# Attention and two feed-forward layers in one launch: query sums and output low parts on another engine, with a new table of positions

## The chip, the cores and the metric

The kernel runs on one core of one Trainium2 chip. The metric is the device time of one execution in microseconds. Before the change it is 699.79 us (median of 3 runs, 699.38 to 701.0).

## The reference

Three stages follow one another, all in fp32. Attention has 2 batches, 8 heads, 1152 keys and a head size of 64; neighbouring queries are averaged in pairs first, so each head has 576 of them:

```
q_pool = q.reshape(B, H, S // 2, 2, D).mean(axis=3)
scores = matmul(q_pool, k^T) / sqrt(D)
attn   = softmax(scores, axis=-1)
x      = matmul(attn, v)            -> 1152 tokens x 512
```

The first feed-forward layer takes x through 512 -> 2048 -> 512 with an ELU between, the second does the same with h * tanh(softplus(h)) between. Query and key inputs are drawn eight times larger than the values.

## The kernel before

**High and low parts.** TensorE's operands are rounded, so the kernel multiplies most operands in two parts: a high part, cast by ScalarE or GpSimd, and a low part, the difference between the value and its high part, taken by VectorE or GpSimd. Where a product needs it, the cross terms of both are added.

**Attention.** Two heads of a batch make a pair n (0 to 7). A pair has 1152 query rows over both heads, in nine tiles of 128 (tile t = 0 to 8; over all pairs s = 9n + t, 72 tiles). For each pair:

- `load_qk` and `load_v` bring the raw rows, `pool_q` (L216) adds the two queries of each pair of rows (tile `qp`, 96 x 768), `turn_q` lets TensorE transpose the sums (`psq`, L233), `split_q` (L244, L246) scales them and makes high and low parts, and `stack_q` (L248) copies them into `QH`, `QL` and `QM` by ten DMAs. The keys go the same way without the sum (`turn_k`, `split_k`, `stack_k`), the values through `split_v` (high by ScalarE L329, low by GpSimd L331).
- For each tile s, `scores` (L356) makes 1152 scores a row, 896 in the buffer `wide` and 256 in `rest`. `maxima` takes the maximum on VectorE (L363, L366), `exps` the exponentials and their sums on ScalarE (`rest` L378, `wide` L380). `turn` (L411) transposes the probabilities in three chunks, `split_a` makes high and low parts: for half of the chunks on ScalarE and VectorE (L436, L438), for the chunks in the list `PP['pool']` by a copy on ScalarE (`whole`, L426, two buffers) and two instructions on GpSimd (L226, L227). The list goes by 3t + c and has no chunk of tile 8. `values` (L451) multiplies with the values.
- At a pair's end `reciprocals` sends 1/sum through DRAM into a broadcast tile `R`, `join` (L464, L466) collects `xf`, and `finish` does three things: the product with `R` (link 0, L474, GpSimd), the high part `xh` (link 1, L476, ScalarE), and the low part `xl` (link 2, L478, VectorE).

**Weights.** The weights arrive as 64-bit numbers. Each 128 x 512 block is decoded by one ScalarE instruction (L602) and four of VectorE (L603, L604, L605, L607). For seventeen blocks this runs during attention, and the result is stored to DRAM and loaded again later; a few more are decoded for use at once.

**Feed-forward.** `up` (L772) and `down` (L792) run over chunks of tokens and 16 blocks of 128 hidden columns. The first chunk of the first layer needs tokens of batch 0 only, pairs 0 to 3.

**The order of the work.** In attention the order of the instructions on every engine is written out: `run` gives each piece of work a position, counted in tiles, sorts all of them, and emits them in that order. The positions stand in the table `PP['x']`: a key such as `m` (first maximum) or `p` (the sum of a pair's queries) holds an offset that is added to s, or to 9n for a pair. Keys with `@0` hold for pair 0 and the preparation of pair 1, `@7` for pair 7. An instruction waits in its engine's queue until its inputs are there, and all behind it wait too. In the feed-forward stage the order on ScalarE and VectorE is that of emission. All DMAs are issued on SP's queue.

Of the kernel before, what the change touches and what calls it, by code (L numbers as in the profile page):

```python
# [15 lines left out]
ALU = mybir.AluOpType  # L16
# [48 lines left out]
    'pl': ['xm'],  # L65
# [72 lines left out]
class Attention:  # L138
# [77 lines left out]
    def pool_q(self, n, heads=slice(0, 2)):  # L216
        if n not in self.qp:
            self.qp[n] = self.tmp.tile([PQ, NQ, 2, D], F32, name="qp", bufs=1)
        qr = self.rawqk[n][0][:, heads]
# [665 lines left out]
```

## Time and profile before

| | |
|---|---|
| median of 3 runs | 699.79 us |
| the profiled execution | 699.27 us, span 697.2 us |
| granted TensorE clock | 0.999 |
| TensorE busy | 674.0 us, 97% of the span |
| VectorE busy | 610.8 us, 88% |
| ScalarE busy | 479.0 us, 69% |
| GpSimd busy | 267.1 us, 38% |
| chain that ended last | TensorE 59%, VectorE 18%, ScalarE 10%, DMA 6%, GpSimd 2% |

In the profile PE is TensorE's matmul, PEld its weight load, DVE is VectorE, ACT ScalarE, POOL GpSimd, and SP the engine that issues the DMAs. The span is the time from the first to the last instruction; the profiled execution's own time is 2.1 us above it. A row of a view by stretch gives start and end, the length, and then the busy microseconds of PE, PEld, DVE, ACT and POOL. A share of busy time is a mean over stages, so the rows below look at the attention stage, up to about 287 us, by itself. Matmuls overlap, so a busy TensorE isn't a TensorE at its peak. The chain of waits is followed back from the last instruction: at each step to what released it, or to the instruction before it on its engine.

### The profile page before, as it was taken

To read this page: it belongs to the slowest core of one execution; us is meant where nothing else is said; L and a number is where in the kernel's file an instruction comes from. 1 tells how busy PE (TensorE), PEld (TensorE's weight loads), DVE (VectorE), ACT (ScalarE), POOL (GpSimd) and SP (SyncE) were. 2 spreads that over 40 slices of the span, in tenths; PEclk is the share of its full clock that TensorE was granted. 3 is DMA by queue.
4 is the path that set the end of the run, shared out by engine and by line. 5 is a ranking of instruction groups with operands and counts; after the bars stand their busy time and mean duration, and the time that the engine had idled before them with its cause. 6 is when DMAs were issued, how large, how long until landed. Compare 5 with 4: busy or idle time off the path is not lost.

```text
span 697.2 us, 11870 instructions
## 1 busy us (share of the span) xinstructions
PE 674.0 (97%) x4006; PEld 602.3 (86%) x4007; DVE 610.8 (88%) x1111; ACT 479.0 (69%) x1125; POOL 267.1 (38%) x308
## 2 busy tenths in 40 slices
PE   8999999999999988999999999999989999999996
PEld 5888988888888877788889999999978999999995
DVE  5999999999999999788798887886999988888884
ACT  5999999999899989765665443666655554445443
POOL 2797788878787868352210000224130000000000
PEclk9999999999999999999999999999999999999999
DMA  6977677758675642546546666565120010001001
GB/s 175 222 186 190 186 196 203 178 130 243 183 177 151 164 128 62 184 136 210 171 149 188 186 214 206 173 191 171 47 77 17 0 46 1 0 1 47 1 0 45
DMA packets 66492, 91.24 MB, mean 131 GB/s; under 512 B 24376, under 2 KB 40832, under 8 KB 66432
## 3 DMA queue, kind: packets, MB, share of 16 engines
q1 hardware_dynamic: 66432, 90.50, 46.9%
q8 instruction: 31, 0.51, 0.3%
q14 instruction: 29, 0.24, 0.1%
HBM read 60.56 MB, written 12.88 MB: 105 GB/s over the span
## 4 chain that ended last, share of the span: by engine, by line
PE 59%; DVE 18%; ACT 10%; DMA 6%; issue 3%; POOL 2%; SPq 0%; ACTq 0%; DVEq 0%; POOLq 0%
PE acc L792 23%; PE up L772 23%; PE psv L451 4%; PE pst L411 4%; PE wide L356 3%; DVE neg L366 3%; DVE wt L605 2%; DVE tl L438 2%; DMA raw<-in_moe_w_out_dram 2%; ACT a L380 2%; DVE wt L607 2%; DMA raw<-in_moe_w_in_dram 2%; DVE wt L603 1%; ACT th L436 1%; ACT wt L602 1%
## 5 line engine op out<-in xcount | busy, mean ns | idle before, releaser
L624 POOL TENSOR_TENSOR wl<-wt,wh 128x512 fp32r<-128x512 f32 x34 | 45.3, 1342 | 194.7 <-ACT wh L622 165.6
L227 POOL TENSOR_TENSOR tl<-whole,th 128x384 fp32r<-128x384 f32 (+1 forms) x112 | 112.9, 1008 | 9.3
L772 PE MATMUL up<-xh,wl 128*128 128x384 f32 (+2 forms) x336 | 113.0, 336 | 0.0
L772 PE MATMUL up<-xh,wh 128*128 128x384 f32 (+2 forms) x336 | 112.9, 336 | 0.0
L772 PE MATMUL up<-xl,wh 128*128 128x384 f32 (+2 forms) x336 | 112.8, 336 | 0.0
L411 PE MATMUL pst<-ident,a 128*128 128x128 f32 x648 | 101.9, 279 | 8.5 <-DVE tl L438 3.2
L411 PEld LDWEIGHTS pst<-ident,a 128*128 128x128 f32 x648 | 73.3, 140 | 25.4 <-DVE tl L438 6.1
L451 PE MATMUL psv<-th,vs 128*128 128x320 f32 (+1 forms) x288 | 85.1, 317 | 1.9 <-DVE tl L438 1.6
L226 POOL TENSOR_SCALAR th<-whole 128x384 fp32r<-128x384 f32 (+1 forms) x112 | 65.2, 582 | 42.7 <-ACT whole L426 41.7
L451 PE MATMUL psv<-tl,vs 128*128 128x320 f32 (+1 forms) x288 | 79.0, 295 | 0.0
L366 DVE TENSOR_REDUCE neg<-wide 128x1 f32<-128x898 f32 x72 | 78.0, 1083 | 0.5
L380 ACT ACTIVATE a<-wide,neg 128x896 f32<-128x896 f32 x72 | 73.9, 1026 | 2.5 <-DVE neg L366 2.3
L602 ACT ACTIVATE wt<-raw 128x512 f32<-128x512 f32 x64 | 43.1, 676 | 39.7 <-DMA raw<-in_moe_w_out_dram 28.2
L745 ACT ACTIVATE e<-n 128x384 f32<-128x384 f32 x48 | 25.2, 526 | 65.0 <-DVE n L744 65.0
L772 PEld LDWEIGHTS up<-xh,wh 128*128 128x128 f32 x336 | 63.3, 189 | 4.0
L772 PEld LDWEIGHTS up<-xl,wh 128*128 128x128 f32 x336 | 63.3, 188 | 4.0
L772 PEld LDWEIGHTS up<-xh,wl 128*128 128x128 f32 x336 | 63.3, 188 | 2.2
L438 DVE TENSOR_TENSOR tl<-pst,th 128x384 fp32r<-128x384 f32 (+1 forms) x128 | 59.8, 495 | 3.4 <-ACT th L436 2.0
L792 PE MATMUL acc<-gh,wl 128*128 128x512 f32 (+2 forms) x180 | 60.4, 336 | 0.0
L451 PEld LDWEIGHTS psv<-th,vs 128*128 128x128 f32 x288 | 54.4, 189 | 4.0 <-issue 1.3
L356 PE MATMUL wide<-ks,qh 128*128 128x448 f32 (+1 forms) x160 | 57.5, 373 | 0.0
L792 PE MATMUL acc<-gl,wh 128*128 128x512 f32 (+2 forms) x168 | 56.6, 337 | 0.1
(128 smaller groups left out, 1769.1 us busy)
## 6 DMA issues: line engine op xcount, KB each, us to landing
raw<-in_moe_w_out_dram SPq DMA_DIRECT2D x32, 512.0 KB, 3.8
raw<-in_moe_w_in_dram SPq DMA_DIRECT2D x32, 512.0 KB, 4.4
w<-wt SPq DMA_DIRECT2D x40, 256.0 KB, 4.4
wt<-w SPq DMA_DIRECT2D x40, 256.0 KB, 3.1
kr<-in_k_dram SPq DMA_DIRECT2D x16, 288.0 KB, 5.2
vr<-in_v_dram SPq DMA_DIRECT2D x8, 576.0 KB, 6.1
qr<-in_q_dram SPq DMA_DIRECT2D x7, 576.0 KB, 5.0
qh<-tqh SPq DMA_DIRECT2D x28, 144.0 KB, 5.1
```

Of the source, the lines that this page charges most:

```text
L226: nc.gpsimd.tensor_scalar(hi, x, 1.0, 1.0, op0=ALU.mult, op1=ALU.mult)
L227: nc.gpsimd.tensor_tensor(lo, x, hi.bitcast(F32), op=ALU.subtract)
L356: nc.tensor.matmul(dst, w[:], x[:, cols], start=(o == 0), stop=(o == len(ops) - 1))
L366: nc.vector.tensor_reduce(neg[:], wide[:, :, :WW + 1], axis=AX.XY, op=ALU.max, negate=True)
L380: nc.scalar.activation(a[:, :2 * WW].rearrange("p (c x) -> p c x", c=2), wide[:, :, :WW], AF.Exp, bias=neg[:], accum_out=self.sums[n][:, t ...
L411: nc.tensor.transpose(ps[:, i * P:(i + 1) * P], a[:, j * P:(j + 1) * P], self.ident[:])
L438: nc.vector.tensor_tensor(l, src[:, :, x0:x0 + w], h.bitcast(F32), op=ALU.subtract)
L451: nc.tensor.matmul(ps[:, :w], self.VS[n % 2][:, h, j].rearrange("p a d -> p (a d)"), t[:, j, :w], start=(c == 1), stop=(c == 2 * NKT))
L602: lambda: nc.scalar.activation(t[:], high.bitcast(F32), AF.Abs),
L624: e.tensor_tensor(l[:], t[:], h[:].bitcast(F32), op=ALU.subtract)
L772: nc.tensor.matmul(ps[:, :z], w, x, start=(o == 0), stop=(o == len(ops) - 1))
L792: nc.tensor.matmul(ps[:, :x.shape[1]], a, x, start=(i == 0 and o == 0), stop=(i == NFF - 1 and o == 2))
```

## The change

Three edits. The list `'pl'` gets `'xl'`, which sends link 2 of `finish` (L478, the low part of the attention's output, 128 x 576, once a pair) to GpSimd. `pool_q` runs on GpSimd for pairs 1 to 7; pair 0 keeps its two half sums on VectorE. And every offset of the position table has a new value; most shift by less than half a tile.

```diff
-    'pl': ['xm'],
+    'pl': ['xm', 'xl'],
...
-        'W': -0.9652, 'R': -1.0096, 'm': -0.303, 'M': 0.3113, 'e': 0.8476, 'E': 0.6177, 'T0': 0.9667, 'T1': 0.9894, 'T2': 1.2926, 'H0': 1.2651,
-        'H1': 1.4181, 'H2': 1.8235, 'L0': 1.6365, 'L1': 1.695, 'L2': 2.0604, 'f0': 12.6577, 'f1': 13.6176, 'f2': 14.1898, 'lq': -2.6801, 'lv': 0.5421,
-        'p': 0.8401, 'sq': 6.1802, 's0': 6.5617, 's1': 9.5077, ...
...
-        ... 'jd3': 12.6342, 'rec0': 9.964, ...
+        'W': -0.8185, 'R': -0.7929, 'm': -0.1468, 'M': 0.2871, 'e': 1.0106, 'E': 0.622, 'T0': 1.0969, 'T1': 1.1479, 'T2': 1.4158, 'H0': 1.2645,
+        'H1': 1.4197, 'H2': 1.8762, 'L0': 1.5754, 'L1': 1.7679, 'L2': 2.0558, 'f0': 13.0233, 'f1': 13.4493, 'f2': 13.9188, 'lq': -2.5868,
+        'lv': 0.6571, 'p': 0.9219, 'sq': 4.0105, 's0': 6.7254, 's1': 7.815, ...
...
+        ... 'jd3': 12.403, 'rec0': 9.9947, ...
...
-        self.nc.vector.tensor_tensor(out, qr[:, :, :, 0, :], qr[:, :, :, 1, :], op=ALU.add)
+        (self.nc.gpsimd if n > 0 else self.nc.vector).tensor_tensor(out, qr[:, :, :, 0, :], qr[:, :, :, 1, :], op=ALU.add)
```

The line that `'xl'` switches is not in the diff; it stands in `finish`:

```python
(nc.gpsimd if 'xl' in PP['pl'] else nc.vector).tensor_tensor(xl, xf[:], xh.bitcast(F32), op=ALU.subtract)
```

## Rows read from the trace of the kernel before

**Rows 1.** Stretches: us, each engine's busy us (instructions), granted clock, DMA share, GB/s.

```profile
20.00:280.00 260.00, 248.10 (x1715) 219.86 (x1712) 251.10 (x430) 241.81 (x624) 206.28 (x249) 1.00 0.67 172
0.00:287.00 287.00, 271.51 (x1847) 236.16 (x1849) 270.43 (x468) 259.28 (x664) 215.25 (x269) 1.00 0.67 172
540.00:680.00 140.00, 140.00 (x704) 126.95 (x703) 120.41 (x242) 69.47 (x146) 1.29 (x1) 1.00 0.04 12
```

**Rows 2.** Chain of waits, 0 to 287 us: shares; steps (start, us, what).

```profile
by line: PE psv L451 10.6%; PE pst L411 9.9%; PE wide L356 6.8%; DVE neg L366 6.6%; issue 6.1%; DVE tl L438 5.8%; ACT a L380 4.1%; DVE wt L605 3.8%; ACT th L436 3.3%; DVE wide L363 3.1%; ACT whole L426 2.9%; PE rest L356 2.6%; DMA raw<-in_m
...
145.16 1.00 DVE neg L366
147.23 1.18 PE psv L451 x8
```

**Rows 3.** Chain of waits: its steps on the moved instructions.

```profile
16.84 0.87 DVE qp L221
46.23 1.15 DVE qp L221
...
231.20 0.82 DVE xl L478
266.75 1.28 DVE xl L478
```

**Rows 4.** Waits, 0 to 287 us: who for whom, us, times, longest.

```profile
POOL th L226 <- ACT whole L426: 41.7, 39, 3.1
PEld rest L356 <- ACT a L378: 2.9, 17, 0.2
```

**Rows 5.** VectorE by line, 0 to 287 us (| busy us, mean ns |).

```profile
L607 DVE SCALAR_TENSOR_TENSOR wt<-raw,wt 128x512 int32<-128x512 int32 x20 | 19.5, 974 | 0.1
L605 DVE SCALAR_TENSOR_TENSOR wt<-raw,wt 128x512 int32<-128x512 int32 x20 | 19.2, 960 | 0.1
L604 DVE TENSOR_SCALAR wt<-wt 128x512 int32<-128x512 int32 x21 | 13.7, 653 | 0.1
L603 DVE TENSOR_SCALAR wt<-wt 128x512 f32<-128x512 f32 x21 | 11.6, 553 | 0.0
L478 DVE TENSOR_TENSOR xl<-xf,xh 128x576 fp32r<-128x576 f32 x7 | 8.4, 1203 | 0.0
L221 DVE TENSOR_TENSOR qp<-qr 96x768 f32<-96x768 f32 x7 | 8.3, 1180 | 0.0
```

**Rows 6.** Order of time near 292 us: start, us, instruction, [idle before].

```profile
294.85 1.28 POOL L624 TENSOR_TENSOR wl<-wt,qr 128x512 fp32r<-128x512 f32 x1 [3.24 <-ACT qr L622]
...
292.36 0.76 DVE L478 TENSOR_TENSOR xl<-xf,xh 128x576 fp32r<-128x576 f32 x1 [0.42 <-ACT xh L476]
```

**Rows 7.** Groups by line, GpSimd, 0 to 287 us.

```profile
L227 POOL TENSOR_TENSOR tl<-whole,th 128x384 fp32r<-128x384 f32 x96 | 102.3, 1066 | 8.0
L474 POOL TENSOR_TENSOR xf<-xf,R 128x576 f32<-128x576 f32 x7 | 9.9, 1420 | 5.0 <-DVE xf L466 3.7 <-DMA R<-rdram 1.3
```

**Rows 8.** Order of time: GpSimd's holes, TensorE's turn of the sums.

```profile
50.85 0.51 POOL L226 TENSOR_SCALAR th<-whole 128x384 fp32r<-128x384 f32 x1 [0.81 <-ACT whole L426]
...
49.45 0.41 PE L233 MATMUL psq<-ident,qp 96*128 96x96 f32 x3
...
149.62 0.51 POOL L226 TENSOR_SCALAR th<-whole 128x384 fp32r<-128x384 f32 x1 [1.99 <-ACT whole L426]
...
150.95 0.41 PE L233 MATMUL psq<-ident,qp 96*128 96x96 f32 x3
```

**Rows 9.** Groups by line, VectorE, 385 to 435 us, where GpSimd is idle.

```profile
L605 DVE SCALAR_TENSOR_TENSOR wt<-raw,wt 128x512 int32<-128x512 int32 x14 | 9.7, 692 | 0.5
L607 DVE SCALAR_TENSOR_TENSOR wt<-raw,wt 128x512 int32<-128x512 int32 x13 | 9.0, 691 | 0.4
L604 DVE TENSOR_SCALAR wt<-wt 128x512 int32<-128x512 int32 x14 | 6.0, 427 | 0.5
L603 DVE TENSOR_SCALAR wt<-wt 128x512 f32<-128x512 f32 x14 | 6.0, 426 | 7.2 <-ACT wt L602 7.0
```

112 rows, old and new, of the table PP are left out of this document.

## The prediction

> **What bounds the kernel now.** I read the busy time by stretch first. From 540 to 680 us TensorE is busy for 140.00 of 140 us: the two feed-forward layers stream matmuls and nothing of the change is in them but one subtraction. The attention stage, up to about 287 us, is another matter: TensorE 271.51, VectorE 270.43, ScalarE 259.28 and GpSimd 215.25 busy us [rows 1]. Three engines stand within 4% of each other, so this stage has no single bound, and the share of busy time alone doesn't say what VectorE's relief is worth.
>
> Next the chain of waits over that stage. It names lines of TensorE and VectorE in turn [rows 2]; the VectorE lines that the row names (neg 6.6, tl 5.8, wt L605 3.8, wide 3.1) make 19.3% of it. In order of time it changes hands inside each pair of heads: at 145.16 us a VectorE maximum is on it, from 147.23 us TensorE streams its own work [rows 2]. So a microsecond taken off VectorE counts in some stretches and not in others.
>
> Third, which of the moved instructions stand on that chain: two of the seven sums (0.87 and 1.15 us) and two of the seven subtractions in the stage (0.82 and 1.28 us) [rows 3], 4.1 us together. Last the waits: GpSimd's largest is for ScalarE's copies of the transposed probabilities, 41.7 us in 39 places; TensorE's for the freed rest of the scores is small, 2.9 us in 17 [rows 4]. GpSimd has room, if not always at the right place.
>
> **The change part by part.** *Off VectorE.* Pair 0 keeps its two half sums there. Seven sums of 96x768 go, 8.3 us, and the subtractions of pairs 0 to 6, 8.4 us [rows 5]: 16.7 us in the attention stage. The eighth subtraction starts at 292.36 us, takes 0.76 us and comes behind an idle 0.42 us [rows 6], in the stage that TensorE streams: nothing. Of the 16.7 us, 4.1 us are on the chain. The other 12.6 us are worth something where a queue behind them reaches the chain later: between nothing and all of it. I take the 19.3% of the chain that named VectorE lines hold, 2.4 us. Sum: -6.5 us. Where it goes, TensorE's stream and ScalarE's copies are late next.
>
> *Onto GpSimd.* A subtraction has the form of the product beside it, 128x576: 1.42 us. For the sum of 768 columns no row exists. From 384 columns at 1.066 us to 576 at 1.420 us [rows 7] another 192 columns add 0.354 us, so 1.77 us; in proportion to columns it would be 1.89. I take 1.8. It reads neighbouring rows of queries in steps, and no GpSimd row shows such a read, so I keep 3.6 us, double, as the upper end. The stage gets 7 x 1.8 + 7 x 1.42 = 22.5 us, and GpSimd stands at some 238 us of it, 84%.
>
> What hides this? In the new order a sum stands between GpSimd's last split of one pair of heads, from tile 7, and its first of the next; tile 8, between them, gives GpSimd no splits, by the list 'pool'. The trace shows the hole: GpSimd idle for 1.99 us before 149.62, so from 147.63; the sum would end at 149.43, and TensorE turns the sums from 150.95 [rows 8]. Cover 1.5 us. In the pair before 50 us the hole opens only at 50.85 - 0.81 = 50.04 us while TensorE turned at 49.45 [rows 8]: the sum would end at 51.84, 2.4 us late, if the queue stood as before. Behind the sum GpSimd holds the splits that feed the products with the values, and behind TensorE's transpose everything of TensorE's. The xl subtraction has no reader in this stage; behind it wait splits only, some 1.4 us each time, and it now comes after ScalarE's xh cast in GpSimd's queue, with two other splits put between: I cost that wait at nothing, against up to 0.7 us if the cast is late. The eighth one adds 1.42 us at 292 us, before low parts of weights that start at 294.85 after 3.24 us of idling [rows 6]: hidden.
>
> *What VectorE pays back.* Where GpSimd is busy, VectorE's weight decoding is slower. Means of its four lines in the stage are 553, 653, 960 and 974 ns [rows 5]; in the stretch from 385 to 435 us they are 426, 427, 692 and 691 ns [rows 9]. With 21, 21, 20 and 20 instructions that is 2.7 + 4.7 + 5.4 + 5.7 = 18.5 us that go with GpSimd's 215 busy us. 22.5 us more in proportion: 1.9 us. Bounds: nothing, if the holes fall beside PSUM reads; twice that, 3.8 us, since the added instructions are longer than the splits. I take 1.9 us and count it in full: +1.9.
>
> *The order.* Sorted, the two tables give nearly the same VectorE queue. Three shifts stand out. TensorE now emits the wide scores ahead of the rest; ScalarE frees the wide half first, so part of the 2.9 us [rows 4] can go, or as much can come as a wait for the wide buffer: -2.9 to +2.9, I take 0. The product with 1/sum goes later behind VectorE's join (12.66 to 13.02 in tiles, the join 12.63 to 12.40): GpSimd had waited for it, off the chain, 0. On SP's queue the ten query copies of each pair come some two tiles earlier and the second key copy 1.7; both still stand after their producers and ahead of their readers by more than a tile, so 0, against a microsecond a pair if SP should hold a later load behind them (7 us, the upper end). Stores of decoded weights move back by up to 7 tiles; their readers are in the feed-forward stage, 0.
>
> Sum: -6.5 + 1.9 = -4.6 us. The profiled run took 699.27 us, of which 697.2 are the span; it lies 0.5 us under the median of the three, 699.79. The sum made against it gives 694.7, on the median's footing 695.2 us.
>
> A rule speaks against this change: by the Trainium skill ("SBUF — State Buffer", section "SBUF: two separate sides"), VectorE and GpSimd share a port pair as a lock held for a whole instruction, so a VectorE instruction with two SBUF inputs waits for the end of a GpSimd one that reads SBUF. The excess of the decoding lines in this trace agrees (974 against 691 ns), and by it the added work would cost more than in proportion, as the second rival works out.
>
> **The rivals.** *Slower: GpSimd's queue decides.* TensorE takes its instructions in order, so if the sum is late, the transposes, the scores and the values behind it wait. For: at 49 us the hole comes 2.4 us late; the splits feed the values too. Against: at 150 us there is 1.5 us to spare, and the new order puts the sum in the hole. It decides from a mean wait above 4.6 / 7 = 0.7 us a pair. At the mean of the two places, (0 + 2.4) / 2 = 1.2 us, seven pairs cost 8.4 us: 695.2 + 8.4 = 703.6.
>
> *No change: long GpSimd instructions hold VectorE.* 82 decoding instructions meet 22.5 us more of GpSimd in 287, a share of 7.8%; the rest of an instruction of 1.4 to 1.8 us is 0.8 us in the mean: 82 x 0.078 x 0.8 = 5.1 us instead of 1.9. -6.5 + 5.1 = -1.4: 698.4, and with a small loss from the order 700. For: the 18.5 us of today. Against: the sum stands beside PSUM reads.
>
> *More: VectorE was the bound after all.* It is at 270.43 / 287 = 94.2%. If ScalarE, untouched by the change, takes over at that same share, the stage ends at 259.28 / 0.942 = 275.2, 11.8 us sooner: 688.0. For: VectorE is busy for 251.10 of the 260 us from 20 to 280 [rows 1]. Against: the stretches that TensorE streams.
>
> *The change doesn't take:* pair 0's sums (at 7 us) stay on VectorE, as the code says; the rest moves by plain engine names, so this has no chance worth a number.
>
> **How the numbers follow.** The forecast, some 691 to 698, has 0.54; the rival above it in gain 0.13, no change 0.14, slower 0.19. This kernel's measurement tells 0.2%, 1.4 us, from no change. Faster is 0.54 + 0.13 = 0.67, same 0.14, slower 0.19. The range goes from the large gain, 688.0, to 703.0, just under the priced loss: some 0.08 is left out below and 0.10 above.
>
> **What would show it.** Right: the attention stage ends some 4 to 5 us sooner; VectorE's busy time there is down by about 15 us; sums on GpSimd at about 1.8 us; hardly any wait of TensorE for the sums; the feed-forward stage as long as before. Wrong in the payback: decoding lines well over 1 us in the mean. Wrong in the cover: TensorE's turn of the sums, or its products with the values, waiting for GpSimd by several us. Wrong in the whole: the stage's end unmoved with VectorE's idle time grown by what left it, which would say that TensorE and ScalarE held the stage.

## The result: 705.79 us, slower by about 1%

The changed kernel takes 705.79 us (median of 4 runs, 705.48 to 706.38), beside 699.59 us for the kernel before on the same chip (median of 4, 696.83 to 701.0). The ratio is 1.0096, with an interval of 1.0075 to 1.0117: 6.7 us slower, where 4.6 us faster was forecast, and outside the range. The profiled execution took 705.76 us, its span 704.0.

First the row that says in which stage the time went, of the kernel after: the first product of the feed-forward stage (columns: count, shortest, median and longest ns, first and last start in us).

```profile
L772 PE MATMUL up<-xh,wh x336: 278/334/394, 293.5 to 689.8; 128*128 128x384 f32 x112, 128*128 128x512 f32 x28, 128*128 128x256 f32 x28
```

In the kernel before, this line starts first at 287.0 and last at 683.0 us. So the attention stage has become 6.5 us longer, and what follows is as long as it was (396.3 against 396.0 us). Next the stretches of after that answer to [rows 1], the attention stage up to its own end.

```profile
0.00:293.50 293.50, 271.33 (x1846) 239.88 (x1848) 258.71 (x454) 258.87 (x662) 233.17 (x283) 0.99 0.64 167
540.00:680.00 140.00, 140.00 (x703) 126.71 (x702) 121.38 (x244) 69.30 (x147) 2.42 (x2) 1.00 0.04 12
```

VectorE is busy for 258.71 us instead of 270.43, 11.7 us less, and GpSimd for 17.9 us more. TensorE and ScalarE work as long as before (271.33 against 271.51, 258.87 against 259.28). What has grown is the part of the stage in which TensorE does nothing: 287.0 - 271.5 = 15.5 us before, 293.5 - 271.3 = 22.2 us after. That difference is the whole loss. The chain of waits of after, up to the same end, by line:

```profile
by line: PE pst L411 11.3%; PE psv L451 11.1%; PE wide L356 7.2%; issue 6.7%; DVE neg L366 5.4%; DVE tl L438 5.1%; ACT a L380 4.6%; ACT th L436 4.0%; ACT whole L426 3.5%; DVE wt L603 3.3%; DMA ql<-tql 3.1%; ACT a L378 2.6%; DVE wt L605 2.4%
```

Against [rows 2] no line has taken over: neg (6.6%) and tl (5.8%) have a little less. New among the first are the decoding line L603 with 3.3% and the DMA of the query copies (ql<-tql) with 3.1%. By the rows of the waits the engines stand 0.6 us in all for query and key copies, so SP's queue, which the prediction allowed up to 7 us, doesn't show as the cause. The waits of after (who for whom, us, times, longest), beside [rows 4]:

```profile
POOL th L226 <- ACT whole L426: 31.9, 34, 3.3
...
DVE tl L438 <- ACT th L436: 9.9, 23, 0.9
PEld pst L411 <- ACT whole L426: 8.2, 20, 1.4
...
PEld psv L451 <- DVE tl L438: 4.0, 4, 1.3
...
PEld rest L356 <- ACT a L378: 2.5, 6, 0.7
```

The relieved engine waits: VectorE's low parts of the probabilities stand 9.9 us for ScalarE's high parts. TensorE waits a little more in several places. The lines of the moved and the decoding instructions, VectorE and then GpSimd of after (| busy us, mean ns | idle before):

```profile
L605 DVE SCALAR_TENSOR_TENSOR wt<-raw,wt 128x512 int32<-128x512 int32 x21 | 18.6, 884 | 0.1
L603 DVE TENSOR_SCALAR wt<-wt 128x512 f32<-128x512 f32 x21 | 16.1, 769 | 0.6 <-ACT wt L602 0.4
L607 DVE SCALAR_TENSOR_TENSOR wt<-raw,wt 128x512 int32<-128x512 int32 x19 | 15.9, 837 | 0.1
...
L604 DVE TENSOR_SCALAR wt<-wt 128x512 int32<-128x512 int32 x21 | 11.2, 532 | 0.2
```

```profile
L221 POOL TENSOR_TENSOR qp<-qr 96x768 f32<-96x768 f32 x7 | 12.8, 1830 | 0.0
L478 POOL TENSOR_TENSOR xl<-xf,xh 128x576 fp32r<-128x576 f32 x7 | 10.6, 1518 | 0.0
L474 POOL TENSOR_TENSOR xf<-xf,R 128x576 f32<-128x576 f32 x7 | 10.4, 1488 | 2.2 <-DVE xf L466 2.1
```

A sum takes 1.83 us on GpSimd. Of the four decoding lines one became slower than in [rows 5], L603, from 553 to 769 ns in the mean; the other three became faster.

One place stands out when the ends of the tiles of both traces are laid beside each other: near 50 us after loses some 3 us within three tiles. The order of time there (start, us, instruction, [idle before]):

```profile
48.78 1.84 POOL L221 TENSOR_TENSOR qp<-qr 96x768 f32<-96x768 f32 x1
...
49.09 2.29 DVE L603 TENSOR_SCALAR wt<-wt 128x512 f32<-128x512 f32 x1
...
50.57 0.52 POOL L226 TENSOR_SCALAR th<-whole 128x384 fp32r<-128x384 f32 x1
...
50.93 0.41 PE L233 MATMUL psq<-ident,qp 96*128 96x96 f32 x3
...
51.30 1.07 DVE L366 TENSOR_REDUCE neg<-wide 128x1 f32<-128x898 f32 x1
...
52.40 0.49 DVE L466 TENSOR_TENSOR xf<-psv,avlo 64x320 f32<-64x320 f32 x1
52.46 1.01 ACT L380 ACTIVATE a<-wide,neg 128x896 f32<-128x896 f32 x1 [1.74 <-DVE neg L366]
...
52.95 0.39 PE L451 MATMUL psv<-th,vs 128*128 128x256 f32 x1 [1.61 <-DVE xf L466]
...
54.00 0.90 PE L411 MATMUL pst<-ident,a 128*128 128x128 f32 x3 [0.55 <-DVE tl L438]
```

The sum itself is in time: it ends at 50.62, and TensorE turns it at 50.93 without a wait. But the decoding step beside it takes 2.29 us instead of 0.43 in quiet, and the maximum and the join behind it on VectorE come late: ScalarE stands 1.74 us, TensorE 1.61 and then 0.55 us. What follows for TensorE stands in two stretches of the same trace (granted clock in the third column from the end):

```profile
53.95:57.36 3.41, 3.36 (x16) 3.37 (x17) 2.89 (x5) 2.00 (x5) 1.66 (x2) 0.50 0.27 60
58.00:62.00 4.00, 3.83 (x29) 3.53 (x28) 3.44 (x6) 3.60 (x10) 2.94 (x4) 1.00 0.44 122
```

For 3.41 us the granted clock is 0.50, the 1.2 GHz level, with TensorE busy: 16 matmul records in that time against 29 in the 4.00 us at 58.

### The profile page after: what moved, and what is told of

It reads as the page before. It is cut to its first block, busy times and chain, and to the rows that moved or that the text cites. A ratio compares the mean times of both kernels' runs of the same rounds, so it can differ in the third digit from the quotient of the medians.

```text
span 704.0 us, 11859 instructions
## 1 busy us (share of the span) xinstructions
PE 674.1 (96%) x4006; PEld 606.2 (86%) x4007; DVE 598.3 (85%) x1096; ACT 479.0 (68%) x1125; POOL 286.8 (41%) x323
## 4 chain that ended last, share of the span: by engine, by line
PE 66%; DVE 15%; ACT 11%; DMA 3%; issue 3%; POOL 1%; SPq 0%; DVEq 0%; ACTq 0%; POOLq 0%
PE acc L792 26%; PE up L772 26%; PE pst L411 5%; PE psv L451 5%; PE wide L356 3%; DVE neg L366 2%; DVE tl L438 2%; ACT a L380 2%; ACT th L436 2%; DVE wt L603 2%; ACT whole L426 1%; DVE wt L605 1%; DMA ql<-tql 1%; ACT a L378 1%; DVE wt L607 1%
## 5 line engine op out<-in xcount | busy, mean ns | idle before, releaser
L411 PE MATMUL pst<-ident,a 128*128 128x128 f32 x648 | 105.7, 280 | 11.2 <-DVE tl L438 2.9
L451 PE MATMUL psv<-th,vs 128*128 128x256 f32 (+1 forms) x288 | 88.8, 325 | 5.8 <-DVE tl L438 3.1
L451 PE MATMUL psv<-tl,vs 128*128 128x256 f32 (+1 forms) x288 | 80.6, 297 | 0.0
L380 ACT ACTIVATE a<-wide,neg 128x896 f32<-128x896 f32 x72 | 73.6, 1023 | 4.5 <-DVE neg L366 4.3
L226 POOL TENSOR_SCALAR th<-whole 128x384 fp32r<-128x384 f32 (+1 forms) x112 | 60.4, 539 | 32.6 <-ACT whole L426 31.9
L438 DVE TENSOR_TENSOR tl<-pst,th 128x384 fp32r<-128x384 f32 (+1 forms) x128 | 61.4, 500 | 11.9 <-ACT th L436 9.9
L356 PE MATMUL wide<-ks,qh 128*128 128x448 f32 (+1 forms) x160 | 61.7, 400 | 0.0
L792 PE MATMUL acc<-gh,wl 128*128 128x512 f32 (+2 forms) x180 | 60.4, 336 | 0.0
L436 ACT CAST th<-pst 128x384 fp32r<-128x384 f32 (+1 forms) x128 | 53.7, 447 | 8.2 <-PE pst L411 7.0
```

The costliest lines, as they stand in the source:

```text
L226: nc.gpsimd.tensor_scalar(hi, x, 1.0, 1.0, op0=ALU.mult, op1=ALU.mult)
L356: nc.tensor.matmul(dst, w[:], x[:, cols], start=(o == 0), stop=(o == len(ops) - 1))
L380: nc.scalar.activation(a[:, :2 * WW].rearrange("p (c x) -> p c x", c=2), wide[:, :, :WW], AF.Exp, bias=neg[:], accum_out=self.sums[n][:, t ...
L411: nc.tensor.transpose(ps[:, i * P:(i + 1) * P], a[:, j * P:(j + 1) * P], self.ident[:])
L436: nc.scalar.copy(h, src[:, :, x0:x0 + w])
L438: nc.vector.tensor_tensor(l, src[:, :, x0:x0 + w], h.bitcast(F32), op=ALU.subtract)
```

## The experiments

Losses in us are the ratio less 1, times 699. Ratios are against the kernel before on the same chip, with the interval of 95%. By that measure the change as it was made costs 6.7 us.

**The parts one by one.** *e1, both instructions on GpSimd, in the old order:*

```diff
-    'pl': ['xm'],
+    'pl': ['xm', 'xl'],
...
-        self.nc.vector.tensor_tensor(out, ...)
+        (self.nc.gpsimd if n > 0 else self.nc.vector).tensor_tensor(out, ...)
```

> The table of positions of before, with the sums of pairs 1 to 7 and the output's low parts on GpSimd. Before is 699.6 us, after 705.8. Theory 'table' (the new positions cost the time, the engines are worth what was forecast): 694 to 697 us. Theory 'engines' (long GpSimd instructions hold VectorE's decoding, as at 49 us of the trace of after, where an L603 took 2.29 us beside a sum): 703 to 706. Theory 'worthless' (ScalarE and TensorE hold the attention stage, so relief of VectorE buys nothing): 699 to 701.

Measured: 709.89 us, 1.0133 (1.0109 to 1.0157), 9.3 us slower, so worse than with the new order.

*e2, the new order alone, both instructions on VectorE:*

```diff
     'x': {
-        'W': -0.9652, 'R': -1.0096, 'm': -0.303, 'M': 0.3113, ...
+        'W': -0.8185, 'R': -0.7929, 'm': -0.1468, 'M': 0.2871, ...
...
```

> The new table of positions with both steps back on VectorE. 'Table': 706 to 712 us, slower than after, since VectorE has its 16.7 us back. 'Engines': 698 to 701, as before. 'Worthless': some 704 to 706, as after, with the granted clock falling or not as the stalls of TensorE near 50 us go or stay.

Measured: 707.03 us, 1.0107 (1.0086 to 1.0127), 7.5 us slower. The new offsets cost by themselves what the whole change costs; moving the instructions on top of them takes 0.8 us off, which the intervals don't tell from nothing. The attention stage of this kernel, to its end:

```profile
0.00:295.50 295.50, 272.10 (x1848) 238.70 (x1849) 264.96 (x469) 259.02 (x662) 212.20 (x269) 1.00 0.63 166
```

TensorE works as long as ever, 272.10 us, and is idle for 23.4 us instead of 15.5; with VectorE's and GpSimd's work where it was, the order alone has made these stops. Neither the half clock nor the long L603 near 49 us is among them: the granted clock is 1.00 in the whole stage, and with the sum on VectorE that L603 takes 0.42 us, at 50.88. The row of TensorE's waits that grew most is that for the low parts of the keys:

```profile
PE pst L411 <- DVE kl L276: 3.4, 5, 1.3
```

The kernel before has no such row, and after has 0.8 us in 2 places; what else grew is spread over many rows.

*The old order with the sums alone, e3, and with the low part alone, e4:*

```diff
-        self.nc.vector.tensor_tensor(out, ...)
+        (self.nc.gpsimd if n > 0 else self.nc.vector).tensor_tensor(out, ...)
```

> The old table, the sums alone on GpSimd. 'Table': 697 us, half of the relief. 'Engines': 701 to 704, since the sums (1.83 us each) are the longest instructions of GpSimd. 'Worthless': 699 to 701.

```diff
-    'pl': ['xm'],
+    'pl': ['xm', 'xl'],
```

> The old table, the output's low parts alone on GpSimd. 'Table': 697 us. 'Engines': 700 to 702 (1.43 us each, the form of the product that GpSimd has already). 'Worthless': 699 to 701.

Measured: 698.29 us for the sums, 0.9985 (0.9971 to 1.0000), and 710.08 us for the low part, 1.0152 (1.0126 to 1.0178). So the sums on GpSimd cost nothing and give next to nothing, and the loss of e1 is the low part's. Its waits, from the trace of e1:

```profile
DVE xf L466 <- POOL xl L478: 14.3, 6, 2.5
...
PEld psk L264 <- DVE xf L466: 9.2, 6, 2.0
PE psk L264 <- DVE xf L466: 6.9, 5, 1.7
```

The same three rows, with the same numbers, stand in the trace of e4. VectorE waits in six places, 2.4 us each, for the subtraction on GpSimd, though it reads nothing of it. It is about to write what GpSimd still reads: the tile `xf` has one buffer (`bufs=1`), and the first join (L466) of the next pair writes it. One of the six, in order of time:

```profile
99.65 1.41 POOL L478 TENSOR_TENSOR xl<-xf,xh 128x576 fp32r<-128x576 f32 x1
...
101.09 0.41 DVE L466 TENSOR_TENSOR xf<-psv,avlo 64x256 f32<-64x256 f32 x1 [2.38 <-POOL xl L478]
...
101.56 0.55 PE L264 MATMUL psk<-ident,kr 128*128 128x128 f32 x3 [1.18 <-DVE xf L466]
...
103.82 0.58 PE L356 MATMUL rest<-ks,qh 128*128 128x256 f32 x1
```

The low part ends at 101.06, the join starts 0.03 us later after an idle of 2.38, and TensorE, whose next transpose waits for the join, has stood for 1.18 us. From 103.72 the granted clock is at 0.50 for 3.41 us here too; the scores at 103.82 take 0.58 us, where the same product of the tile before, at 99.07, took 0.39.

**The buffer.** If the cause is the buffer, it goes when GpSimd's subtraction reads another one. The product with 1/sum is written into `R`, which it reads anyway, and both later steps read `R`; the engines and the old order stay as in e1 (this is e5):

```diff
-            (nc.gpsimd ...).tensor_tensor(xf[:], xf[:], self.R[n][:], op=ALU.mult)
+            (nc.gpsimd ...).tensor_tensor(self.R[n][:], xf[:], self.R[n][:], op=ALU.mult)
...
-            nc.scalar.copy(xh, xf[:])
+            nc.scalar.copy(xh, self.R[n][:])
...
-            (nc.gpsimd ...).tensor_tensor(xl, xf[:], xh.bitcast(F32), op=ALU.subtract)
+            (nc.gpsimd ...).tensor_tensor(xl, self.R[n][:], xh.bitcast(F32), op=ALU.subtract)
```

> The old table with both steps on GpSimd, as the run that took 709.9 us, but the product with 1/sum is written into R and not back into xf; the high and low parts read it there. So the next pair's join no longer waits for the low part. Theory 'xf' (the 11 us that the low part costs on GpSimd under the old table is VectorE's join waiting for the one xf buffer, 14.3 us in 6 places): 697 to 699 us. Theory 'engines' (GpSimd's longer work holds VectorE's decoding): 707 to 710.

Measured: 698.57 us, 0.9992 (0.9974 to 1.0009). The 9.3 us are gone, and no row of that trace has the join wait for GpSimd. This is also the cleanest trial of the idea: both instructions off VectorE, the old order, and no wait of the join for GpSimd. Its attention stage in one row:

```profile
0.00:286.30 286.30, 269.91 (x1848) 235.99 (x1849) 258.23 (x454) 258.86 (x664) 232.86 (x283) 1.00 0.66 173
```

VectorE is busy for 258.23 us, 12.2 less than in [rows 1], and the stage is 0.7 us shorter. The relief itself is worth 0.6 us (from a gain of 1.8 to a loss of 0.6).

**Is VectorE's load worth anything?** The sharpest form leaves work out. *e13, the kernel before, whose low part is not taken for pairs 0 to 6; it is set to zero at the start:*

```diff
+        nc.gpsimd.memset(xl[:].bitcast(F32), 0.0)
...
-        if link == 2:
+        if link == 2 and n == 7:
```

> The kernel before without the low parts of the output of pairs 0 to 6 (xl stays zero there, filled once by GpSimd at the start): VectorE has 8.4 us less to do, GpSimd nothing more inside the stage, and the join waits for nothing. Theory 'VectorE bounds' (as in my forecast): 694 to 696. Theory 'worthless' (ScalarE and TensorE hold the stage): 698 to 699.5.

*e14, the kernel before, in which ScalarE's high parts of the values are not taken from pair 2 on; the buffers keep those of pairs 0 and 1:*

```diff
-            nc.scalar.copy(hi, x)
+            if n < 2:
+                nc.scalar.copy(hi, x)
```

> The kernel before without ScalarE's casts of the values' high parts for pairs 2 to 7 (the buffers keep those of pairs 0 and 1): ScalarE has 18 x 0.52 = 9.4 us less to do, VectorE what it had. Theory 'ScalarE bounds the attention stage': 691 to 694. Theory 'no engine alone bounds it; the order of each tile's handing over does': 697 to 699.5.

*e15, both are left out:*

> Both left out of the kernel before: the output's low parts of pairs 0 to 6 (8.4 us of VectorE) and the casts of the values' high parts of pairs 2 to 7 (9.4 us of ScalarE). Theory 'VectorE and ScalarE hold it together': 691 to 694 even if each alone gives nothing. Theory 'handing over' or TensorE's own stream: 696.5 to 699.

Measured: 698.96 us, 0.9995 (0.9981 to 1.0010); 699.84 us, 1.0009 (0.9994 to 1.0023); 698.97 us, 0.9995 (0.9982 to 1.0009). The stretch from 20 to 280 us of the last, to be laid beside [rows 1]:

```profile
20.00:280.00 260.00, 247.26 (x1715) 219.93 (x1713) 243.00 (x423) 235.63 (x606) 203.55 (x249) 1.00 0.67 172
```

VectorE has lost 8.1 us of 251.10 and ScalarE 6.2 of 241.81, and TensorE does 247.26 us of work in the same 260 us as before, 248.10. Its short waits stay as well (the line numbers here are two higher):

```profile
PEld pst L413 <- ACT whole L428: 4.5, 16, 1.1
...
PEld rest L358 <- ACT a L380: 2.9, 17, 0.2
```

Both rows have the same numbers in the same stretch of the kernel before, the second in [rows 4]. So these waits don't come from the amount of work on VectorE and ScalarE. I read them as the handing over between engines in a written order, which less work elsewhere in the tile doesn't shorten. That reading is argued, not shown: no run takes work off TensorE, which is busy for 95% of this stretch.

**What in the new order costs?** Here parts of one table were put into the other. *e6, the old order with the new positions of the finish (f0 to f2) and of the first join (ja0, jd0), the plain keys and those with @0 and @7, both instructions on GpSimd:*

```diff
-  'f0': 12.6577, 'f1': 13.6176, 'f2': 14.1898, ... 'ja0': 5.1737, 'jd0': 5.404
+  'f0': 13.0233, 'f1': 13.4493, 'f2': 13.9188, ... 'ja0': 5.4535, 'jd0': 5.7019
```

> The old table with both steps on GpSimd, and only the positions of the finish (f0 to f2) and of the first join (ja0, jd0) from the new one: the low part 0.27 tile earlier, the next join 0.3 later. Theory 'xf': most of the 11 us comes back, 698 to 702. If what the new table costs lies in those positions themselves: 705 to 707. 'Engines': 707 to 710.

Measured: 703.71 us, 1.0067 (1.0044 to 1.0091). Half of e1's loss is gone: the low part comes earlier, the join later, and no row of the waits has the join wait for GpSimd. In the profiled execution (702.62 us) what is left sits in one place, where the product comes late:

```profile
267.05 0.67 ACT L476 CAST xh<-xf 128x576 fp32r<-128x576 f32 x1 [2.62 <-POOL xf L474]
268.15 0.31 PEld L411 LDWEIGHTS pst<-ident,a 128*128 128x128 f32 x3 [3.00 <-ACT whole L426]
268.16 0.55 PE L411 MATMUL pst<-ident,a 128*128 128x128 f32 x3 [2.63 <-ACT whole L426]
```

ScalarE waits 2.62 us for GpSimd, the copy behind it on ScalarE is late, and TensorE stands 2.63 us for that.

*After with the old positions of the weight decoding (e7), of the plain keys of a tile, W, R, m, M, e, E, T, H and L (e8), of the last pair (e10):*

```diff
-  'cs0ld': 16.9128, 'cs0co0': 19.2847, ... 'gs2co0': 76.1736
+  'cs0ld': 17.1323, 'cs0co0': 19.0557, ... 'gs2co0': 75.4841
```

> The changed kernel with the positions of the weight decoding from the old table. If the new table's 7 to 8 us come from decoding steps that meet a sum on GpSimd (an L603 of 2.29 us at 49 us, with TensorE's clock at half from 54 to 57 us): 699 to 702. If they come from the positions of the tiles' own work: 704 to 707.

```diff
-  'W': -0.8185, 'R': -0.7929, 'm': -0.1468, ...
+  'W': -0.9652, 'R': -1.0096, 'm': -0.303, ...
```

> The changed kernel with the positions of each tile's own work (scores, maxima, exponentials, transposes, splits) from the old table, so that TensorE emits the rest of the scores ahead of the wide ones again. If the new table's 7 to 8 us come from there: 698 to 702. If from elsewhere: 704 to 708.

```diff
-  'W@7': -0.8086, 'R@7': -0.8238, 'm@7': -0.1533, ...
+  'W@7': -0.8184, 'R@7': -0.8515, 'm@7': -0.3486, ...
```

> The changed kernel with the old positions for pair 7. Theory 'ends': 703.5 to 704.5, since after loses some 1.2 to 1.8 us in the last pair. Theory 'everywhere': 705 to 706.

Measured: 716.24 us, 1.0242 (1.0214 to 1.0270), for the decoding, and 712.72 us, 1.0211 (1.0184 to 1.0238), for the last pair. The second gives the old positions back and loses another 8 us: at the seam between the last two pairs TensorE waits 1.85 us, until 255.46, and the granted clock is at 0.50 for 3.41 us from 256.31. With the plain keys of a tile, tile 9's rest scores come, at the seam between pairs 0 and 1, ahead of tile 7's exponentials (positions 7.99 and 8.09) and are what these then read; its runs spread from 740.63 to 1146.77 us, and nothing is read from them. I take one thing from the three: halves of the two tables need not fit together, so a part that is put back doesn't tell what it costs where it was.

*e9, after with the old positions of the opening (pair 0, the first tiles, the preparation):*

```diff
-  'W@0': -0.9004, 'R@0': -0.7427, ... 'ip1': -7.232, ... 'R_0': -0.2782, ...
+  'W@0': -1.0338, 'R@0': -0.9461, ... 'ip1': -7.8619, ... 'R_0': -0.4983, ...
```

> The changed kernel with the old positions for pair 0, for the preparation of pair 1 and for the opening. The trace of after is 1.6 us behind before when tile 9's exponentials end, and 4.6 by tile 12. Theory 'ends' (the new table loses at the start and in the last pair, not in the pairs between): 701 to 704. Theory 'everywhere' (the new order costs in every pair): 704.5 to 706.

*e12, after with four positions of one decoded block moved back, so that L603 at 49 us comes behind the maximum and the join:*

```diff
-  'cs13co1': 9.9421, 'cs13co2': 10.7477, 'cs13co3': 10.776, 'cs13co4': 11.1089
+  'cs13co1': 10.456, 'cs13co2': 10.7912, 'cs13co3': 11.2618, 'cs13co4': 11.9824
```

> The changed kernel with the four VectorE steps of one decoding chain (cs13) at their old positions, 0.04 to 0.9 tile later, so that the first no longer stands beside pair 2's sum on GpSimd. Theory 'collision' (that sum held an L603 for 2.29 us, the next maximum came late, TensorE stood and its clock fell to half for 3.4 us): 702 to 703.5, and no stretch at half clock. Otherwise 705 to 706.

*e16, both of these:*

> The changed kernel with the old opening (pair 0, preparation of pair 1) and the four decoding steps of cs13 at their old places. If the two losses found so far (3.2 and 2.7 us) are separate, they add up: 699.5 to 701. If the old opening gains only because it moves the same collision away: 702 to 703.

Measured: 702.64 us, 1.0058 (1.0040 to 1.0076); 703.04 us, 1.0065 (1.0047 to 1.0083); both 704.67 us, 1.0079 (1.0060 to 1.0098). Each alone gives back over 2 us of the 6.7, and together they give back 1.2, which the intervals don't tell from nothing. So neither theory of e16 held. Nor are e9 and e12 two separate gains: in the trace of e9 the long L603 is gone as well, for it runs at 47.53 us, 0.22 us ahead of the sum, and takes 0.55. The order of time at 49 us with the block moved, beside that of after:

```profile
48.63 1.83 POOL L221 TENSOR_TENSOR qp<-qr 96x768 f32<-96x768 f32 x1
...
48.96 1.08 DVE L366 TENSOR_REDUCE neg<-wide 128x1 f32<-128x898 f32 x1
...
50.60 0.61 DVE L603 TENSOR_SCALAR wt<-wt 128x512 f32<-128x512 f32 x1
```

The same sum runs beside a maximum that reads PSUM, which takes 1.08 us, its mean over the 72 in after (1.086); L603 takes 0.61. TensorE's longest stop from 49 to 58 us is 0.49 us, and the clock from 53.95 to 57.36 is at 1.00. With the old opening as well another place breaks:

```profile
64.77 1.40 POOL L474 TENSOR_TENSOR xf<-xf,R 128x576 f32<-128x576 f32 x1 [6.16 <-DMA R<-rdram]
...
66.20 0.67 ACT L476 CAST xh<-xf 128x576 fp32r<-128x576 f32 x1 [4.00 <-POOL xf L474]
...
68.29 0.55 PE L411 MATMUL pst<-ident,a 128*128 128x128 f32 x3 [3.38 <-ACT whole L426]
```

GpSimd reaches the product too early and stands 6.16 us for the broadcast of 1/sum, ScalarE 4.00 us for GpSimd, TensorE 3.38 us for ScalarE. Then the clock is at 0.50 from 69.76 to 73.17.

No version beats the kernel before. The sums alone (698.29 us) and both with the product in `R` (698.57 us) are 0.15 and 0.08% below it, with intervals that reach 1.

## Why the prediction was wrong

Two terms of the sum failed. The order was put at 0 and costs 7.5 us; the relief of VectorE was put at -6.5 us and is worth 0.3 to 1.0 us in the runs that keep the old order (e13, e5, e3).

**"Off VectorE", -6.5 us: failed.** The instructions went, 11.7 us net in the stage, and the time didn't follow: 0.6 us in e5, 0.3 in e13, with intervals that end before 2, and 0.8 us between e2 and after in the new order, which is not clear of nothing. The step took instructions that stand on the chain of waits as worth their length, and 19.3% of the rest besides. The chain shows who was last in that execution. When that one is taken away, the next is late by nearly as much, as I read it: in [rows 1] TensorE has 248.10 of 260 us, and its waits are short and many. The last of my signs of a wrong forecast, the end unmoved and VectorE's idle time grown by what left it, is what e5, e13 and e15 show. A smaller slip of the reading: TensorE and ScalarE stand 4.5% apart in [rows 1], not within 4%.

**"The xl subtraction has no reader in this stage ... I cost that wait at nothing": right in number, by luck.** It has no reader, but it has a writer behind it. In the old order that costs 10.6 us (e4), and by e5 against e1 the cost goes with the buffer. In the changed kernel the cost doesn't arise: there the first join comes later and the subtraction earlier, and VectorE's join (L466) waits for ScalarE only, 7.0 us in 13 places, never for GpSimd. That the new positions of the finish and the join are enough for it is shown by e6. So this term is no part of the 6.7 us; I followed what reads `xl`, and didn't ask who next writes `xf`.

**"The order", 0 (-2.9 to +2.9): failed, and this is the loss.** It is +7.5 us by e2. I compared two sorted queues of VectorE and looked for large shifts; offsets that differ by tenths of a tile decide which of two instructions stands first in each of five queues. Which positions make the 7.5 us stays open. By the ends of the wide exponentials (L380), one trace each, e2 is behind the kernel before by 2.3 us at the end of pair 0, 3.6 of pair 1, 4.9 of pair 2, 6.5 of pair 3 and 8.4 of pair 7. The one piece that is shown, the long L603 at 49 us, which costs after 2.2 us (e12, just clear of the noise), is made by order and engine together: it needs the new offsets and the sum on GpSimd, and neither e2 (longest L603 1.49 us) nor e3 (1.17) has it. The old opening gives 2.7 us back (e9), but moves the same L603 away, so what the opening costs by itself isn't shown.

**Onto GpSimd, 22.5 us: right.** 12.8 + 10.6 = 23.4 us in the stage. GpSimd's busy time grew by 17.9 us only, above all since the high parts (L226) fell from 65.2 to 60.4 us. The sum came between my two extrapolations, 1.77 and 1.89; so no cost of its reading in steps shows.

**What VectorE pays back, +1.9 us: right in sign, its size depends on the order.** Over the quiet means of [rows 9] the four lines of after lie 21 x 192 + 19 x 146 + 21 x 105 + 21 x 343 ns = 16.2 us, against 18.5 before. But that compares two orders. With the new order and both instructions on VectorE (e2: 860, 858, 513 and 564 ns in the same order of lines) they lie 11.6 us over, so moving the instructions raised this by 4.6 us there; in the old order (e5: 985, 963, 652 and 558 ns) they lie 18.8 us over, 0.3 us more than before. The largest single piece came in one place: 1.9 us on one L603, and the late maximum behind it. This is where the lock rule of the Trainium skill ("SBUF — State Buffer", section "SBUF: two separate sides") is borne out in kind: L603 starts 0.31 us after the sum and ends 0.76 us after it. The rule names VectorE instructions with two SBUF inputs and those in a mode that uses both ports; L603 has one SBUF input, so only the second can apply, and no row shows the mode. By the rule it would wait for the sum's end at 50.62 and then take its quiet 0.43, to 51.05; measured is 51.38, which is 0.29 us after the end of the next GpSimd instruction (50.57 to 51.09). So it reads as held by both, one behind the other. The same page of the Trainium skill (section "Who interferes with whom") has a reduction never held in this way on trn2; the maximum beside the same sum in e12, 1.08 us, agrees. My rival that built on the rule priced the payback at 5.1 us; in the new order that is near the 4.6, but the loss is there without it, in e2.

**The slower rival: its sign, not its mechanism.** It had TensorE's turn of the sums wait for GpSimd. In the source view of the sum of after nobody waits for it. In the old order (e3) there is one such wait, at 49.11 us, where I had placed it, of 0.33 us for TensorE instead of 2.4. The large-gain rival, VectorE as the bound, is refuted by e5 and e13. The no-change rival had -1.4 us for the engines, close to the 0.8 us between e2 and after, but by e13 for another reason: the relief itself is worth little.

**The feed-forward stage as long as before: right**, 396.3 against 396.0 us from the first product to the last.

## What to carry to other kernels

When an instruction goes to another engine, look not only for who reads its output but for who next writes its input: a tile with one buffer turns a step without readers into a wait. An engine that is busy for 94% of a stage need not be its bound when another one, with its short waits, fills the stage by itself; leaving the work out in a trial costs one run and says what the relief can be worth at most. In queues that run in order, a new set of positions is a change of its own and has to be timed by itself, without the edit that it came with.

## What the runs showed that I had not expected

A stop of TensorE can cost more than its length. Each stretch at half clock that I followed lasts 3.41 us and begins in or behind stops: 1.61 and 0.55 us (after, 53.95), 1.18 us with smaller ones behind it (e1, 103.72), 2.63 us (e6, 269.59), 3.38 us (e16, 69.76), 3.59 us (e7, 270.90). In such a stretch a score matmul of 256 columns, the first of its tile, takes 0.58 us instead of 0.39. The length of one stop doesn't decide it alone: e1 has stops of 1.55 and 1.65 us, e5 a single one of 1.7 us, the kernel before one of 1.1, and no such stretch follows them.

A decoding step with one SBUF input (L603) can be held by GpSimd: 2.29 us for 0.43 to 0.61, while a maximum that reads PSUM beside the same sum takes its usual 1.08 us. It isn't the only one. In after eleven of the 21 take over 0.6 us, ten of them start while a GpSimd instruction runs, and these end 0.27 to 0.29 us after the end of a GpSimd instruction. One of them:

```profile
87.79 1.01 POOL L227 TENSOR_TENSOR tl<-whole,th 128x384 fp32r<-128x384 f32 x1
...
87.91 1.18 DVE L603 TENSOR_SCALAR wt<-wt 128x512 f32<-128x512 f32 x1 [0.21 <-ACT wt L602]
```
